# A decode block over a 537 MB cache: K and V in 4 MB tiles of 32 KB runs, wq loaded whole, w2 on 128 partitions, one K tile split into 120 and 8 partitions

## The chip, the cores and the metric

The kernel runs on one core of one Trainium2 chip. The metric is device time in microseconds (us). The kernel before takes 1334.83 us, the median of 3 runs (1334.46 to 1336.64). Two runs of this kernel that differ by less than about 0.2% can't be told apart.

An execution that is profiled has a time of its own and a span, from its first to its last instruction. Durations below come from that one execution.

## The reference

One token of each of two sequences goes through an attention block over a cache and then an MLP. All is float32.

```python
B, Sq, D = 2, 1, 512;  H, Sk, Dh = 32, 8192, 128;  F = 1792
y = layernorm(x)
q = (y @ wq) as (B, H, 1, Dh)                      # wq: D x 4096
s = einsum("bhqd,bhkd->bhqk", q, k_cache) * Dh**-0.5
o = einsum("bhqk,bhkd->bhqd", softmax(s), v_cache)
h = x + (o as (B, 1, 4096)) @ wo                   # wo: 4096 x D
z = layernorm(layernorm(h))
out = h + gelu(z @ w1 + b1) @ w2 + b2              # w1: D x F, w2: F x D
```

K and V are 268 MB each; wq and wo are 8.4 MB each, w1 and w2 3.7 MB each. Each byte is used once.

## The kernel before

**Pairs and tiles.** There are 64 pairs of a head and a sequence (`pairs`, L135). The 8192 positions of a pair lie on 128 partitions, 64 to a partition (`NS`), and are worked in two steps of 32 (`CH`, `NC` = 2). `load` (L139) fetches a step's K or V as a tile of 128 partitions x 32 positions x 128 numbers: 2 MB, in which each partition has one run of 16 KB in DRAM. All these tiles, and later w1's and w2's, come from one pool of 9 buffers (`BUFS`), used in turn: a load waits until its buffer's previous tile is done with.

**Queues.** All large loads are issued by SP in the order of the program, each for all 16 DMA engines. The loop (L235) goes over the steps. In step n it issues K of step n, now and then a wo group (`load_wo`, 2 heads, 512 KB) or a wq group (`load_wq`, 4 heads, 1 MB), and V of step n - 3 (`LAG`). The small loads of x, b1 and b2 go by ACT's queue at the start.

**Scores.** q of a head is needed on every partition. `make_q` (L119) makes it for two heads at a time: the normalised x, repeated over 128 columns (`yrep`), is the stationary side, and a slice of the wq group the moving one, so that PSUM holds q on each partition (L124, 8 matmuls a call). DVE multiplies the K tile by q in place (`multiply`, L151). ACT sums 10 of the 32 positions (`by_act`, L156), DVE the other 22 (`by_dve`, L160).

**Softmax.** After both steps of a pair: the row maximum (L167), its transpose on PE (L169), the maximum over all (L173), its spread to all partitions (L175), the exponentials on ACT (L182), and their total (L187).

**Values.** `values` (L194) multiplies the exponentials by V on PE, 8 matmuls for a tile (L199), in four groups of output rows. `gather` copies the result out of PSUM (L205); `head_sum` (L211) and `head_out` (L218) make the head's output, and `project` (L224) applies wo for a head once both sequences are done. `behind` places small DVE work after the next multiply. V of the last step comes as three loads of 16, 8 and 8 positions (L233).

**MLP.** After the loop w1 is loaded as 4 tiles of 128 rows (7 KB runs) and w2 as 4 tiles of 112 partitions (`FP`), with four runs of 2 KB to a partition (L283 to L292). The layer norms run across partitions with matmuls against a constant matrix (`layernorm_t`, L306). w1's 16 matmuls (L341) put the 1792 hidden values on four groups of partitions, 448 each; gelu (L353) is followed by four transposes on PE (L356) and a copy (L358), and w2's 16 matmuls (L362), four to a w2 tile, end in a copy (L365), a sum of the four groups (L367), the residual (L369) and the store.

Of the kernel before, what the change touches and what calls it, by code (L numbers as in the profile page):

```python
# [9 lines left out]
F32 = mybir.dt.float32  # L10
BF16 = mybir.dt.bfloat16
AF = mybir.ActivationFunctionType
ALU = mybir.AluOpType
AX = mybir.AxisListType

P = 128
EPS = 1e-5
HG = 4
QG = 2
CH = 32  # L20
NACT = 10
LAG = 3
BUFS = 9
NG = 4
WARM = 3

# [2 lines left out]
def tile_decode_block(ctx: ExitStack, tc: tile.TileContext, x, k, v, wq, wo, w1, b1, w2, b2, out):  # L29
    nc = tc.nc  # L30
    B, H, SK, DH = k.shape
    D = x.shape[-1]
    F = w1.shape[1]
    NS = SK // P
    NC = NS // CH
    DC = D // P
    FN = F // NG
    FP = FN // NG
    SCALE = DH ** -0.5

    const = ctx.enter_context(tc.tile_pool(name="const", bufs=1))
    wts = ctx.enter_context(tc.tile_pool(name="wts", bufs=2))
    kv = ctx.enter_context(tc.tile_pool(name="kv", bufs=BUFS))
    work = ctx.enter_context(tc.tile_pool(name="work", bufs=3))
    psq = ctx.enter_context(tc.tile_pool(name="psq", bufs=2, space=bass.MemoryType.PSUM))
    psm = ctx.enter_context(tc.tile_pool(name="psm", bufs=3, space=bass.MemoryType.PSUM))
# [2 lines left out]
    x2 = const.tile([B, D], F32, name="x2")  # L49
    nc.scalar.dma_start(x2, x.rearrange("b s d -> (b s) d"))  # L50

    wq_g, wo_g = {}, {}

    def load_wq(g):
        t = wts.tile([P, DC, HG * DH], F32, name="wqg")
        nc.sync.dma_start(
            t, wq[:, g * HG * DH:(g + 1) * HG * DH].rearrange("(c p) n -> p c n", p=P))
        wq_g[g] = t

    def load_wo(g):  # L60
        t = wts.tile([P, QG, D], F32, name="wog")
        nc.sync.dma_start(
            t, wo[g * QG * DH:(g + 1) * QG * DH, :].rearrange("(h p) n -> p h n", p=P))
        wo_g[g] = t

    load_wq(0)
    b1s = const.tile([NG, FN], F32, name="b1s")
    nc.scalar.dma_start(b1s, b1.rearrange("(n f) -> n f", n=NG))
    b2s = const.tile([B, D], F32, name="b2s")
# [3 lines left out]
    ident = const.tile([P, P], F32, name="ident")  # L73
# [11 lines left out]
    sel = const.tile([P, 4], F32, name="sel")  # L85
# [5 lines left out]
    so2 = [psa.tile([P, 512], F32, name=f"so{j}") for j in range(2)]  # L91
# [11 lines left out]
    y2 = const.tile([B, D], F32, name="y2")  # L103
    nc.vector.tensor_scalar(y2, x2, mv[:, 0:1], rs, op0=ALU.subtract, op1=ALU.mult)

    def transpose_rows(src):
        pt = psm.tile([P, DC, B], F32, name="sm")
        for c in range(DC):
            nc.tensor.transpose(pt[:, c, :], src[:, c * P:(c + 1) * P], ident[:B, :B])
        return pt  # L110

    ypt = transpose_rows(y2)
    yrep = const.tile([P, B, DC, P], F32, name="yrep")
    for b in range(B):
        nc.vector.tensor_copy(yrep[:, b], ypt[:, :, b:b + 1].to_broadcast([P, DC, P]))

    qps = {}

    def make_q(h):  # L119
        g, hh = divmod(h, HG)  # L120
        t = psq.tile([P, B, QG, DH], F32, name="qps")
        for b in range(B):
            for c in range(DC):
                nc.tensor.matmul(t[:, b], yrep[:, b, c, :], wq_g[g][:, c, hh * DH:(hh + QG) * DH],  # L124
                                 start=(c == 0), stop=(c == DC - 1))
        for j in range(QG):
            qps[h + j] = t[:, :, j, :]

# [5 lines left out]
    acc = psa.tile([P, DC, B], F32, name="acc")  # L134
    pairs = [(h, b) for h in range(H) for b in range(B)]  # L135
    NP = len(pairs)
    ST, PT, LT, OT = {}, {}, {}, {}

    def load(src, i, s0, n):  # L139
        h, b = pairs[i]  # L140
        t = kv.tile([P, n, DH], F32, name="kv", tag="kv")
        nc.sync.dma_start(  # L142
            t, src[b, h].rearrange("(c p j) d -> c p j d", p=P, j=CH)[s0 // CH, :, s0 % CH:s0 % CH + n])
        return t

    def multiply(i, c, kt):
        h, b = pairs[i]
        if c == 0:
            ST[i] = work.tile([P, NS], F32, name="s")
        qb = qps[h][:, b, None, :].to_broadcast([P, CH, DH])  # L150
        return nc.vector.tensor_tensor(kt, kt, qb, op=ALU.mult)  # L151

    def by_act(i, c, kt):
        s = ST[i]
        for j in range(CH - NACT, CH):
            nc.scalar.activation(kt[:, j, :], kt[:, j, :], AF.Copy,  # L156
                                 accum_out=s[:, c * CH + j:c * CH + j + 1])

    def by_dve(i, c, kt):
        nc.vector.tensor_reduce(ST[i][:, c * CH:(c + 1) * CH - NACT], kt[:, :CH - NACT, :],  # L160
                                axis=AX.X, op=ALU.add)

    MT, GM, RL, SS, OP = {}, {}, {}, {}, {}

# [29 lines left out]
    def values(i, s0, ns, vt):  # L194
        so = so2[i % 2]
        for j in range(ns // 4):
            u = s0 // 4 + j
            n = u % NG
            nc.tensor.matmul(so[32 * n:32 * n + 4], PT[i][:, 4 * u:4 * u + 4],  # L199
                             vt[:, 4 * j:4 * j + 4, :],  # L200
                             start=(u < NG), stop=(u >= NS // 4 - NG))

    def gather(i):
        SS[i] = work.tile([P, 512], F32, name="ss", bufs=2)
        nc.scalar.activation(SS[i], so2[i % 2], AF.Copy)  # L205
# [14 lines left out]
    def project(i):  # L220
        h, b = pairs[i]
        if b == B - 1:
            for c in range(DC):
                nc.tensor.matmul(acc[:, c, :], wo_g[h // QG][:, h % QG, c * P:(c + 1) * P], OT[h],  # L224
                                 start=(h == 0 and c == 0), stop=(h == H - 1),
                                 skip_group_check=True)

    def behind(m):
        return tc.issue_after(m.ins) if m is not None else nullcontext()

    kstream = [(i, c) for i in range(NP) for c in range(NC)]
    vstream = [(i, c * CH, CH) for i, c in kstream[:-1]]
    vstream += [(NP - 1, NS - CH, CH // 2), (NP - 1, NS - CH // 2, CH // 4), (NP - 1, NS - CH // 4, CH // 4)]  # L233
    maxed, expd, done, projecting = [], [], [], []
    for n in range(len(vstream) + LAG):  # L235
        live = n < len(kstream)
        if live:
            i, c = kstream[n]
            h, b = pairs[i]
            kt = load(k, i, c * CH, CH)  # L240
            if b == 0 and c == 0 and h % QG == 0:
                load_wo(h // QG)
            if b == 0 and c == 1 and h % HG == 1 and h // HG + 1 < H // HG:
                load_wq(h // HG + 1)
        if n >= LAG:
            vt = load(v, *vstream[n - LAG])
        with behind(multiply(i, c, kt) if live else None):
            for j in done:
                head_sum(j)
                head_out(j)  # L250
            for j in expd:
                inverse(j)
            for j in maxed:
                all_max(j)
        projecting, done, expd = done, [], []
        if live:
            by_act(i, c, kt)
        for j in maxed:
            exps(j)
        if live:  # L260
            by_dve(i, c, kt)
        if n >= LAG:
            iv, s0, ns = vstream[n - LAG]
            values(iv, s0, ns, vt)
        for j in maxed:
            total(j)
        expd, maxed = maxed, []
        if live and c == NC - 1:
            row_max(i)
            maxed.append(i)  # L270
            if b == 0 and h % QG == 1 and h + 1 < H:
                make_q(h + 1)
        for j in projecting:
            project(j)
        if n >= LAG and s0 + ns == NS:
            gather(iv)
            done.append(iv)
    for j in done:
        head_sum(j)
        head_out(j)  # L280
        project(j)

    w1s, w2s = [], []  # L283
    for c in range(DC):
        t = kv.tile([P, F], F32, name="w1s", tag="kv")
        nc.sync.dma_start(t, w1[c * P:(c + 1) * P, :])
        w1s.append(t)
    w2v = w2.rearrange("(n q p) d -> q p n d", p=FP, n=NG)
    for q in range(NG):
        t = kv.tile([FP, NG, D], F32, name="w2s", tag="kv")  # L290
        nc.sync.dma_start(t, w2v[q])
        w2s.append(t)  # L292

    junk = const.tile([P, 2], F32, name="junk")
    nc.scalar.activation(junk[:, 0:1], LT[NP - 1], AF.Sqrt)
# [40 lines left out]
    pf = so2[0][:, :FN]  # L336
# [12 lines left out]
    with tc.issue_after(last_ln.ins):  # L349
        nc.vector.tensor_add(hb2, hr, b2s)  # L350

    ff = work.tile([P, FN], F32, name="ff", tag="ss", bufs=2)
    nc.scalar.activation(ff, pf, AF.Gelu_apprx_tanh)  # L353
    ft = psm.tile([FP, NG, P], F32, name="sm")
    for q in range(NG):
        nc.tensor.transpose(ft[:, q, :], ff[:, q * FP:(q + 1) * FP], ident)  # L356
    fT = const.tile([FP, NG, NG, B], F32, name="fT")
    nc.vector.tensor_copy(fT, ft.rearrange("p q (n b) -> p q n b", n=NG)[:, :, :, :B])  # L358
    po = so2[1]
    for q in range(NG):  # L360
        for n in range(NG):
            nc.tensor.matmul(po[32 * n:32 * n + B], fT[:, q, n, :], w2s[q][:, n, :],  # L362
                             start=(q == 0), stop=(q == NG - 1))
    pos = work.tile([P, D], F32, name="pos", tag="ss", bufs=2)
    nc.scalar.activation(pos, po, AF.Copy)  # L365
    pr = psm.tile([B, D], F32, name="sm")
# [29 lines left out]
```

## Time and profile before

| | |
|---|---|
| median of 3 runs | 1334.83 us |
| the profiled execution, its own time | 1337.41 us |
| its span | 1335.6 us |
| read from DRAM | 561 MB, 420 GB/s over the span |
| DMA in the middle (600 to 1200 us) | 430 GB/s |
| K and V loads of 2 MB | 255, landing some 36 us after their issue |
| mean granted TensorE clock | 0.646 |

A line of the page's groups has the program's line, the engine, the operation, what it writes and reads with its shape, how often it occurs, its busy time and its mean in ns, and then how long the engine sat idle before it and what ended that. In a table of stretches, a DMA share of 1.00 means that all 16 DMA engines are occupied. A chain of work is followed back from the last instruction, at each step to what released it.

### The profile page before, as it was taken

The page shows a single profiled execution, that of the slowest core. Times are in us where ns is not written, and L with a number is a line of the kernel's source. Part 1 is how long each engine was busy: PE and PEld are TensorE (multiplying, and loading weights), DVE is VectorE, ACT ScalarE, POOL GpSimd, SP SyncE. Part 2 cuts the span into 40 slices and gives each one's busy share as a digit, 9 for nine tenths or more (in the row PEclk, how much of TensorE's full clock was granted, in tenths as well). Part 3 has the DMA queues.
Part 4 walks back from the last instruction along what each step waited for, and adds up shares of the span by engine and source line. Part 5 has one row for each costly group of instructions (what it writes and reads, how often), then busy time and mean ns, then how long its engine had stood idle before and what let it go on. Part 6 is the DMA issues. An engine that isn't in the chain of part 4 may idle for free.

```text
span 1335.6 us, 11258 instructions
## 1 busy us (share of the span) xinstructions
PE 731.0 (55%) x3501; PEld 304.1 (23%) x3502; DVE 996.3 (75%) x547; ACT 465.5 (35%) x2827; POOL 0.7 (0%) x6
## 2 busy tenths in 40 slices
PE   3465644565455565545555545564554555454566
PEld 2122211223122232221222112231221212221221
DVE  7978877777877877777787777768877777777851
ACT  2433433343333333334333333333433343343331
POOL 0000000000000000000000000000000000000000
PEclk8676566657657565566766666575676766666668
DMA  9999999999999999999999999999999999999994
GB/s 395 431 429 430 431 430 428 430 431 430 429 429 432 430 429 429 430 430 431 430 431 429 431 431 427 430 430 431 429 430 430 430 431 430 431 429 429 432 404 114
DMA packets 48239, 561.73 MB, mean 421 GB/s; under 512 B 4650, under 2 KB 4654, under 8 KB 15412
## 3 DMA queue, kind: packets, MB, share of 16 engines
q1 hardware_dynamic: 48164, 561.01, 99.1%
q8 instruction: 27, 0.44, 0.1%
q14 instruction: 32, 0.26, 0.0%
q10 hardware_dynamic: 16, 0.02, 0.0%
HBM read 561.00 MB, written 0.00 MB: 420 GB/s over the span
## 4 chain that ended last, share of the span: by engine, by line
DMA 85%; DVE 8%; PE 5%; SPq 1%; issue 1%; ACT 0%; DVEq 0%
DMA kv<-in_A_k_cache_dram 46%; DMA kv<-in_A_v_cache_dram 37%; DVE kv L151 5%; PE so L199 3%; DVE s L160 2%; DMA w2s<-in_B_w_dram 2%; PE acc L224 1%; SPq L142 1%; PE qps L124 1%; DMA wqg<-in_A_wq_dram 0%; PE so L362 0%; PE sm L367 0%; DVE ot L218 0%; PE sm L169 0%; ACT L182 0%
## 5 line engine op out<-in xcount | busy, mean ns | idle before, releaser
L151 DVE TENSOR_TENSOR kv<-kv,qps 128x4096 f32<-128x4096 f32 x128 | 565.9, 4421 | 290.3 <-DMA kv<-in_A_k_cache_dram 285.0
L156 ACT ACTIVATE kv<-kv 128x128 f32<-128x128 f32 x1280 | 376.1, 295 | 786.2 <-DVE kv L151 786.2
L199 PE MATMUL so<-kv,pt 128*4 128x512 f32 x2048 | 424.7, 974 | 137.2 <-DMA kv<-in_A_v_cache_dram 137.2
L160 DVE TENSOR_REDUCE s<-kv 128x22 f32<-128x2816 f32 x128 | 392.4, 3066 | 0.1
L156 ACT ACTIVATION_READ_ACCUMULATOR kv<-kv 128x1 f32 x1280 | 238.9, 187 | 0.0
L175 PE MATMUL sm<-gm,srow 1*128 1x1 f32 x128 | 34.1, 333 | 254.6 <-DVE gm L173 254.5
L199 PEld LDWEIGHTS so<-kv,pt 128*4 128x4 f32 x2048 | 51.4, 104 | 322.6 <-issue 179.6
L124 PE MATMUL qps<-wqg,yrep 128*128 128x256 f32 x256 | 82.6, 465 | 49.6 <-issue 24.8
L211 PE MATMUL sm<-sel,ss 128*128 128x1 f32 x512 | 84.5, 286 | 18.8 <-ACT ss L205 18.7
L175 PEld LDWEIGHTS sm<-gm,srow 1*128 1x128 f32 x128 | 28.7, 277 | 283.0 <-DVE gm L173 282.0
L224 PE MATMUL acc<-ot,wog 128*128 128x2 f32 x256 | 56.7, 343 | 59.7 <-DVE ot L218 59.7
L211 PEld LDWEIGHTS sm<-sel,ss 128*128 128x128 f32 x512 | 79.1, 236 | 25.9 <-ACT ss L205 25.9
L224 PEld LDWEIGHTS acc<-ot,wog 128*128 128x128 f32 x256 | 58.6, 326 | 63.8 <-DVE ot L218 61.3
L124 PEld LDWEIGHTS qps<-wqg,yrep 128*128 128x128 f32 x256 | 54.4, 232 | 55.7 <-issue 49.6
L169 PE MATMUL sm<-ident,mx 128*1 128x128 f32 x64 | 21.4, 334 | 64.7 <-DVE mx L167 64.7
L205 ACT ACTIVATE ss<-so 128x512 f32<-128x512 f32 x64 | 38.2, 597 | 48.5 <-PE so L199 47.7
L187 PEld LDWEIGHTS sm<-ls,ones 128*128 128x128 f32 x128 | 25.2, 246 | 96.7 <-ACT pt L182 91.8
L169 PEld LDWEIGHTS sm<-ident,mx 128*1 128x1 f32 x64 | 5.1, 79 | 155.2 <-DVE mx L167 103.7
L187 PE MATMUL sm<-ls,ones 128*128 128x1 f32 x128 | 30.6, 308 | 3.8 <-ACT pt L182 3.2
L182 ACT ACTIVATE pt<-s,nb 128x64 f32<-128x64 f32 x64 | 22.3, 348 | 2.1
L218 DVE TENSOR_SCALAR ot<-sm,rl 128x1 f32<-128x1 f32 x64 | 13.6, 212 | 11.6 <-PE sm L211 11.6
L173 DVE TENSOR_REDUCE gm<-sm 1x1 f32<-1x128 f32 x64 | 17.4, 272 | 2.4 <-PE sm L169 2.4
(70 smaller groups left out, 87.1 us busy)
## 6 DMA issues: line engine op xcount, KB each, us to landing
kv<-in_A_k_cache_dram SPq DMA_DIRECT2D x128, 2048.0 KB, 36.3
kv<-in_A_v_cache_dram SPq DMA_DIRECT2D x127, 2048.0 KB, 35.9
wqg<-in_A_wq_dram SPq DMA_DIRECT2D x8, 1024.0 KB, 36.8
wog<-in_A_wo_dram SPq DMA_DIRECT2D x16, 512.0 KB, 35.2
w1s<-in_B_w_dram SPq DMA_DIRECT2D x4, 896.0 KB, 28.3
w2s<-in_B_w_dram SPq DMA_DIRECT2D x4, 896.0 KB, 23.5
kv<-in_A_v_cache_dram SPq DMA_DIRECT2D x1, 1024.0 KB
kv<-in_A_v_cache_dram SPq DMA_DIRECT2D x2, 512.0 KB, 31.1
```

The costliest lines, as they stand in the source:

```text
L124: nc.tensor.matmul(t[:, b], yrep[:, b, c, :], wq_g[g][:, c, hh * DH:(hh + QG) * DH], start=(c == 0), stop=(c == DC - 1))
L151: return nc.vector.tensor_tensor(kt, kt, qb, op=ALU.mult)
L156: nc.scalar.activation(kt[:, j, :], kt[:, j, :], AF.Copy, accum_out=s[:, c * CH + j:c * CH + j + 1])
L160: nc.vector.tensor_reduce(ST[i][:, c * CH:(c + 1) * CH - NACT], kt[:, :CH - NACT, :], axis=AX.X, op=ALU.add)
L169: nc.tensor.transpose(MT[i], mx, ident)
L175: nc.tensor.matmul(GM[i], srow, gm, start=True, stop=True)
L182: nc.scalar.activation(pt, ST.pop(i), AF.Exp, bias=nb, scale=SCALE, accum_out=ls)
L187: nc.tensor.matmul(RL[i], ones, LT[i], start=True, stop=True)
L199: nc.tensor.matmul(so[32 * n:32 * n + 4], PT[i][:, 4 * u:4 * u + 4], vt[:, 4 * j:4 * j + 4, :], start=(u < NG), stop=(u >= NS // 4 - NG))
L205: nc.scalar.activation(SS[i], so2[i % 2], AF.Copy)
L211: nc.tensor.matmul(OP[i], ss[:, j * DH:(j + 1) * DH], sel[:, j:j + 1], start=(j == 0), stop=(j == 3))
L224: nc.tensor.matmul(acc[:, c, :], wo_g[h // QG][:, h % QG, c * P:(c + 1) * P], OT[h], start=(h == 0 and c == 0), stop=(h == H - 1), skip_gr ...
```

## The change

- **Tiles.** A pair's K or V is one tile of 4 MB, in which a partition holds 64 consecutive positions: one run of 32 KB. The pool has 5 such buffers instead of 9 of 2 MB. The two steps of a pair remain, as halves of the K tile. K of the next pair is issued a pair ahead, V of a pair after it; the matmuls with V of pair i - 1 stand in the second step of pair i. The last pair's K comes as 2 loads, its V as 3.
- **K of pair 62**, the last but one, comes as a load of partitions 0 to 119 and a load of 120 to 127 (`PS`).
- **q.** All of wq is loaded ahead of K, as two 4 MB tiles of the same pool with 32 KB runs. Partition p has rows 4p to 4p + 3 of wq, and x is transposed to match. 32 matmuls of 512 columns make q for all heads at once; two ACT copies put it into SBUF (`q2`), and `make_q` spreads two heads with a 0/1 matrix (`pick`), one matmul for each sequence instead of four.
- **wo** groups keep their size; the load of the next group stands in the step before its first head.
- **w1** is one tile with 4 loads. **w2** is one tile on 128 partitions, partition p holding rows 14p to 14p + 13, in loads of 4, 4, 4 and 2 rows: runs of 8 KB (the last 4 KB). gelu writes its output in the order that 32 x 32 transposes on DVE need, and these replace the four transposes on PE and the copy; w2 takes 14 matmuls instead of 16.

```diff
-HG = 4
+PS = 120
+WG = 2
-LAG = 3
-BUFS = 9
+BUFS = 5
...
+    FT = F // P
...
+    wqv = wq.rearrange("(p r) n -> p r n", r=DC)
+    wqs = []
+    for r in range(0, DC, 2):
+        t = kv.tile([P, 2, H * DH], F32, name="wqs", tag="kv")
+        nc.sync.dma_start(t, wqv[:, r:r + 2, :])
+        wqs += [t[:, 0, :], t[:, 1, :]]
...
+    ypt = psm.tile([P, DC, B], F32, name="sm")
+    for r in range(DC):
+        nc.tensor.transpose(ypt[:, r, :], y2.rearrange("b (p r) -> b r p", r=DC)[:, r, :], ident[:B, :B])
+    yT = const.tile([P, DC, B], F32, name="yT")
+    nc.vector.tensor_copy(yT, ypt)
+    pick = const.tile([P, B, P], F32, name="pick")
+    nc.vector.tensor_copy(pick, sel[:, :B, None].to_broadcast([P, B, P]))
+    QW = H * DH // NG
+    q2 = const.tile([P, QW], F32, name="q2")
+    for r in range(DC):
+        for j in range(QW // 512):
+            for n in range(NG):
+                nc.tensor.matmul(so2[j][32 * n:32 * n + B], yT[:, r, :],
+                                 wqs[r][:, n * QW + j * 512:n * QW + (j + 1) * 512],
+                                 start=(r == 0), stop=(r == DC - 1))
+    for j in range(QW // 512):
+        nc.scalar.activation(q2[:, j * 512:(j + 1) * 512], so2[j], AF.Copy)
...
     def make_q(h):
-        g, hh = divmod(h, HG)
+        n, at = divmod(h * DH, QW)
         t = psq.tile([P, B, QG, DH], F32, name="qps")
         for b in range(B):
-            for c in range(DC):
-                nc.tensor.matmul(t[:, b], yrep[:, b, c, :], wq_g[g][:, c, hh * DH:(hh + QG) * DH],
-                                 start=(c == 0), stop=(c == DC - 1))
+            nc.tensor.matmul(t[:, b], pick[32 * n:32 * n + B, b, :],
+                             q2[32 * n:32 * n + B, at:at + QG * DH], start=True, stop=True)
...
-    def load(src, i, s0, n):
+    def load(src, i, parts):
         h, b = pairs[i]
-        t = kv.tile([P, n, DH], F32, name="kv", tag="kv")
-        nc.sync.dma_start(
-            t, src[b, h].rearrange("(c p j) d -> c p j d", p=P, j=CH)[s0 // CH, :, s0 % CH:s0 % CH + n])
+        t = kv.tile([P, NS, DH], F32, name="kv", tag="kv")
+        for s0, n in parts:
+            rows = src[b, h].rearrange("(p j) d -> p j d", j=NS)
+            for p0, p1 in [(0, PS), (PS, P)] if src is k and i == NP - 2 else [(0, P)]:
+                nc.sync.dma_start(t[p0:p1, s0:s0 + n], rows[p0:p1, s0:s0 + n])
         return t
...
-    kstream = [(i, c) for i in range(NP) for c in range(NC)]
-    vstream = [(i, c * CH, CH) for i, c in kstream[:-1]]
-    vstream += [(NP - 1, NS - CH, CH // 2), (NP - 1, NS - CH // 2, CH // 4), (NP - 1, NS - CH // 4, CH // 4)]
+    whole = [(0, NS)]
+    kt, vt = {}, {}
+    kt[0] = load(k, 0, whole)
+    load_wo(0)
+    steps = [(i, c) for i in range(NP) for c in range(NC)] + [(NP, 0), (NP, 1)]
+    for i, c in steps:
+        live = i < NP
+        if c == 0:
+            if live:
+                h, b = pairs[i]
+            if i + 1 < NP:
+                kt[i + 1] = load(k, i + 1, whole if i + 1 < NP - 1 else [(0, CH), (CH, CH)])
+            if live and b == 1 and (h + 1) % WG == 0 and h + 1 < H:
+                load_wo((h + 1) // WG)
+            if live:
+                vt[i] = load(v, i, whole if i < NP - 1 else [(0, CH), (CH, CH // 2), (CH + CH // 2, CH // 2)])
...
-        if n >= LAG:
-            iv, s0, ns = vstream[n - LAG]
-            values(iv, s0, ns, vt)
+        if c == 1 and i > 0:
+            values(i - 1, 0, NS, vt.pop(i - 1))
...
+    w1t = kv.tile([P, DC, F], F32, name="w1s", tag="kv")
     for c in range(DC):
-        t = kv.tile([P, F], F32, name="w1s", tag="kv")
-        nc.sync.dma_start(t, w1[c * P:(c + 1) * P, :])
+        nc.sync.dma_start(w1t[:, c, :], w1[c * P:(c + 1) * P, :])
-    w2v = w2.rearrange("(n q p) d -> q p n d", p=FP, n=NG)
-    for q in range(NG):
-        t = kv.tile([FP, NG, D], F32, name="w2s", tag="kv")
-        nc.sync.dma_start(t, w2v[q])
+    w2v = w2.rearrange("(p t) d -> p t d", t=FT)
+    w2t = kv.tile([P, FT, D], F32, name="w2s", tag="kv")
+    for t in range(0, FT, NG):
+        nc.sync.dma_start(w2t[:, t:min(t + NG, FT), :], w2v[:, t:min(t + NG, FT), :])
...
-    ff = work.tile([P, FN], F32, name="ff", tag="ss", bufs=2)
-    nc.scalar.activation(ff, pf, AF.Gelu_apprx_tanh)
-    ft = psm.tile([FP, NG, P], F32, name="sm")
-    for q in range(NG):
-        nc.tensor.transpose(ft[:, q, :], ff[:, q * FP:(q + 1) * FP], ident)
-    fT = const.tile([FP, NG, NG, B], F32, name="fT")
-    nc.vector.tensor_copy(fT, ft.rearrange("p q (n b) -> p q n b", n=NG)[:, :, :, :B])
+    ff = work.tile([P, FT, 32], F32, name="ff", tag="ss", bufs=2)
+    nc.scalar.activation(ff, pf.rearrange("p (u t) -> p t u", t=FT), AF.Gelu_apprx_tanh)
+    fT = const.tile([P, FT, 32], F32, name="fT")
+    nc.vector.transpose(fT.rearrange("p t r -> p (t r)"), ff.rearrange("p t u -> p (t u)"))
     po = so2[1]
-    for q in range(NG):
-        for n in range(NG):
-            nc.tensor.matmul(po[32 * n:32 * n + B], fT[:, q, n, :], w2s[q][:, n, :],
-                             start=(q == 0), stop=(q == NG - 1))
+    for t in range(FT):
+        n = t % NG
+        nc.tensor.matmul(po[32 * n:32 * n + B], fT[:, t, :B], w2t[:, t, :],
+                         start=(t < NG), stop=(t >= FT - NG))
```

More of the change, by code (lines that the diff above doesn't have):

```diff
@@ L37, in tile_decode_block @@
     FN = F // NG
-    FP = FN // NG
+    FT = F // P
     SCALE = DH ** -0.5
@@ L50, in tile_decode_block, with load_wo @@
     nc.scalar.dma_start(x2, x.rearrange("b s d -> (b s) d"))
-    wq_g, wo_g = {}, {}
-    def load_wq(g):
-        t = wts.tile([P, DC, HG * DH], F32, name="wqg")
+    wo_g = {}
+    def load_wo(g):
+        t = wts.tile([P, WG, D], F32, name="wog")
         nc.sync.dma_start(
[L57 to L61, printed above, removed]
-        nc.sync.dma_start(
-            t, wo[g * QG * DH:(g + 1) * QG * DH, :].rearrange("(h p) n -> p h n", p=P))
-        wo_g[g] = t
-    load_wq(0)
+            t, wo[g * WG * DH:(g + 1) * WG * DH, :].rearrange("(h p) n -> p h n", p=P))
+        wo_g[g] = t
+    wqv = wq.rearrange("(p r) n -> p r n", r=DC)
[4 more added lines that the diff above has]
+        wqs += [t[:, 0, :], t[:, 1, :]]
     b1s = const.tile([NG, FN], F32, name="b1s")
@@ L110, in transpose_rows @@
         return pt
[L112 to L115, printed above, removed]
+    ypt = psm.tile([P, DC, B], F32, name="sm")
[15 more added lines that the diff above has]
+        nc.scalar.activation(q2[:, j * 512:(j + 1) * 512], so2[j], AF.Copy)
     qps = {}
     def make_q(h):
-        g, hh = divmod(h, HG)
+        n, at = divmod(h * DH, QW)
         t = psq.tile([P, B, QG, DH], F32, name="qps")
         for b in range(B):
-            for c in range(DC):
-                nc.tensor.matmul(t[:, b], yrep[:, b, c, :], wq_g[g][:, c, hh * DH:(hh + QG) * DH],
-                                 start=(c == 0), stop=(c == DC - 1))
+            nc.tensor.matmul(t[:, b], pick[32 * n:32 * n + B, b, :],
+                             q2[32 * n:32 * n + B, at:at + QG * DH], start=True, stop=True)
         for j in range(QG):
@@ L137, in tile_decode_block @@
     ST, PT, LT, OT = {}, {}, {}, {}
-    def load(src, i, s0, n):
+    def load(src, i, parts):
         h, b = pairs[i]
-        t = kv.tile([P, n, DH], F32, name="kv", tag="kv")
-        nc.sync.dma_start(
-            t, src[b, h].rearrange("(c p j) d -> c p j d", p=P, j=CH)[s0 // CH, :, s0 % CH:s0 % CH + n])
+        t = kv.tile([P, NS, DH], F32, name="kv", tag="kv")
[3 more added lines that the diff above has]
+                nc.sync.dma_start(t[p0:p1, s0:s0 + n], rows[p0:p1, s0:s0 + n])
         return t
@@ L150, in multiply @@
         qb = qps[h][:, b, None, :].to_broadcast([P, CH, DH])
-        return nc.vector.tensor_tensor(kt, kt, qb, op=ALU.mult)
+        kc = kt[:, c * CH:(c + 1) * CH, :]
+        return nc.vector.tensor_tensor(kc, kc, qb, op=ALU.mult)
     def by_act(i, c, kt):
         s = ST[i]
-        for j in range(CH - NACT, CH):
-            nc.scalar.activation(kt[:, j, :], kt[:, j, :], AF.Copy,
-                                 accum_out=s[:, c * CH + j:c * CH + j + 1])
+        for j in range((c + 1) * CH - NACT, (c + 1) * CH):
+            nc.scalar.activation(kt[:, j, :], kt[:, j, :], AF.Copy, accum_out=s[:, j:j + 1])
     def by_dve(i, c, kt):
-        nc.vector.tensor_reduce(ST[i][:, c * CH:(c + 1) * CH - NACT], kt[:, :CH - NACT, :],
-                                axis=AX.X, op=ALU.add)
+        a, e = c * CH, (c + 1) * CH - NACT
+        nc.vector.tensor_reduce(ST[i][:, a:e], kt[:, a:e, :], axis=AX.X, op=ALU.add)
     MT, GM, RL, SS, OP = {}, {}, {}, {}, {}
@@ L199, in values @@
             nc.tensor.matmul(so[32 * n:32 * n + 4], PT[i][:, 4 * u:4 * u + 4],
-                             vt[:, 4 * j:4 * j + 4, :],
+                             vt[:, 4 * u:4 * u + 4, :],
                              start=(u < NG), stop=(u >= NS // 4 - NG))
@@ L223, in project @@
             for c in range(DC):
-                nc.tensor.matmul(acc[:, c, :], wo_g[h // QG][:, h % QG, c * P:(c + 1) * P], OT[h],
+                nc.tensor.matmul(acc[:, c, :], wo_g[h // WG][:, h % WG, c * P:(c + 1) * P], OT[h],
                                  start=(h == 0 and c == 0), stop=(h == H - 1),
@@ L229, in behind @@
         return tc.issue_after(m.ins) if m is not None else nullcontext()
-    kstream = [(i, c) for i in range(NP) for c in range(NC)]
-    vstream = [(i, c * CH, CH) for i, c in kstream[:-1]]
-    vstream += [(NP - 1, NS - CH, CH // 2), (NP - 1, NS - CH // 2, CH // 4), (NP - 1, NS - CH // 4, CH // 4)]
+    whole = [(0, NS)]
     maxed, expd, done, projecting = [], [], [], []
[L235 to L244, printed above, removed]
-        if n >= LAG:
-            vt = load(v, *vstream[n - LAG])
-        with behind(multiply(i, c, kt) if live else None):
+    kt, vt = {}, {}
[13 more added lines that the diff above has]
+                vt[i] = load(v, i, whole if i < NP - 1 else [(0, CH), (CH, CH // 2), (CH + CH // 2, CH // 2)])
+        with behind(multiply(i, c, kt[i]) if live else None):
             for j in done:
@@ L256, in tile_decode_block @@
         if live:
-            by_act(i, c, kt)
+            by_act(i, c, kt[i])
         for j in maxed:
@@ L260, in tile_decode_block @@
         if live:
-            by_dve(i, c, kt)
-        if n >= LAG:
-            iv, s0, ns = vstream[n - LAG]
-            values(iv, s0, ns, vt)
+            by_dve(i, c, kt[i])
+        if c == 1 and i > 0:
+            values(i - 1, 0, NS, vt.pop(i - 1))
         for j in maxed:
@@ L274, in tile_decode_block @@
             project(j)
-        if n >= LAG and s0 + ns == NS:
-            gather(iv)
-            done.append(iv)
+        if c == 1 and i > 0:
+            gather(i - 1)
+            done.append(i - 1)
     for j in done:
@@ L281, in tile_decode_block @@
         project(j)
-    w1s, w2s = [], []
+    w1t = kv.tile([P, DC, F], F32, name="w1s", tag="kv")
     for c in range(DC):
-        t = kv.tile([P, F], F32, name="w1s", tag="kv")
-        nc.sync.dma_start(t, w1[c * P:(c + 1) * P, :])
-        w1s.append(t)
-    w2v = w2.rearrange("(n q p) d -> q p n d", p=FP, n=NG)
-    for q in range(NG):
-        t = kv.tile([FP, NG, D], F32, name="w2s", tag="kv")
-        nc.sync.dma_start(t, w2v[q])
-        w2s.append(t)
+        nc.sync.dma_start(w1t[:, c, :], w1[c * P:(c + 1) * P, :])
+    w1s = [w1t[:, c, :] for c in range(DC)]
+    w2v = w2.rearrange("(p t) d -> p t d", t=FT)
+    w2t = kv.tile([P, FT, D], F32, name="w2s", tag="kv")
+    for t in range(0, FT, NG):
+        nc.sync.dma_start(w2t[:, t:min(t + NG, FT), :], w2v[:, t:min(t + NG, FT), :])
     junk = const.tile([P, 2], F32, name="junk")
```

## The prediction

> **What bounds the kernel now.** I read the page from the top: the busy row, the DMA row in 40 slices, the queues, and then the chain that ended last.
>
> ```profile
> PE 731.0 (55%) x3501; PEld 304.1 (23%) x3502; DVE 996.3 (75%) x547; ACT 465.5 (35%) x2827; POOL 0.7 (0%) x6
> ...
> DMA  9999999999999999999999999999999999999994
> ...
> q1 hardware_dynamic: 48164, 561.01, 99.1%
> q8 instruction: 27, 0.44, 0.1%
> ...
> q10 hardware_dynamic: 16, 0.02, 0.0%
> ...
> DMA 85%; DVE 8%; PE 5%; SPq 1%; issue 1%; ACT 0%; DVEq 0%
> ...
> L151 DVE TENSOR_TENSOR kv<-kv,qps 128x4096 f32<-128x4096 f32 x128 | 565.9, 4421 | 290.3 <-DMA kv<-in_A_k_cache_dram 285.0
> ```
>
> The 16 DMA engines are busy in every slice, the chain is DMA for 85%, and DVE, the busiest engine, idles 285 us for K. So bytes set the middle. The last 40 us are another matter; the table of stretches (busy us of PE, PEld, DVE, ACT, POOL, then granted clock, DMA share, GB/s) shows it:
>
> ```profile
> 600.00:1200.00 600.00, 328.65 (x1568) 136.81 (x1572) 459.25 (x240) 213.11 (x1315) 0.00 (x0) 0.64 1.01 430
> 1305.00:1312.00 7.00, 5.36 (x32) 3.25 (x31) 1.84 (x11) 0.89 (x2) 0.00 (x0) 1.00 1.04 220
> 1321.00:1328.00 7.00, 3.54 (x28) 0.53 (x26) 0.54 (x2) 0.00 (x0) 0.00 (x0) 0.98 0.08 30
> ```
>
> Two things stand there. From 1321 to 1328 us a share of 0.08 at 30 GB/s is about one engine of 16: **one engine is late**, and the kernel waits for it alone. And from 1305 to 1312 all engines are occupied at half the bytes (220 against 430): something **slows the packets** there. The chain in order of time says that this stretch is on the path:
>
> ```profile
> 1299.52 5.27 PE so L199 x29
> 1304.79 23.47 DMA w2s<-in_B_w_dram
> 1328.26 0.04 issue
> 1328.30 1.93 PE so L362 x8
> ```
>
> The last w2 piece lands at 1328.3, and 7.3 us of work follow to the span's end at 1335.6 (L362 to 1330.2, the copy pos 0.6, L367's matmuls 1.9, res 0.7, and 2.1 for the store).
>
> The trace also keeps, for every load, when each of the 16 engines reported its share. The last engine is 2.1 us behind the first at 98 us, 5.5 at 499, 9.5 at 902 and 13.6 at 1269, in steps of some 0.6 us about every 45 us. That is the rhythm of q8's 27 fetches of 16 KB (27 x 0.6 = 16 us). The second-latest engine is 6.4 us behind at 1269. So one engine carries the instruction fetches beside its data; it sets the landing of every load.
>
> **The sum.** It follows this late engine.
>
> *Packets.* In the middle, eight K/V loads of 2 MB take 38.90 us; seven and one wo load 35.32; seven and one wq load 36.60. That gives 4.863 us for an engine's 8 packets of 16 KB (0.608 each), 1.28 for the 16 packets of 2 KB of wo, and 2.56 for the 32 of wq (0.080 each). So a packet costs about 0.0046 us plus 0.0368 us a KB. By that, 7 KB cost 0.268, 8 KB 0.306, 32 KB 1.211. K and V are 2048 packets of 16 KB an engine now, 1024 of 32 KB then, if a 32 KB run is one packet: 1024 x 0.0046 = 4.7 us less, and half the reports; I take -5 (bounds: 0 if the run is cut in two, -9 by the packets' own recorded times, 611 ns for 16 KB and 309 for 8 KB). wq: 8 x 2.56 = 20.5 now, 16 x 1.211 = 19.4 then: -1.1. L124's 512 PE instructions (256 matmuls, 256 weight loads) become about 256, which is one 16 KB fetch fewer: -0.6. Together -6.7 before the last V part.
>
> *The tail's slow stretch.* The late engine ends V's last 512 KB at 1304.1; its own lag of 13.5 over the first engine's 1288.7 would put it at 1302.2. Then the four w1 loads end at 1308.8, 1313.2, 1316.7 and 1319.1, though 32 packets of 7 KB cost 8.6 us by the sum above: 1302.2 + 8.6 = 1310.8, so 8.3 us are lost. In the packet records w1's take 272 ns until w2's begin at 1298 and some 500 while both are in flight; w2's own take 130 to 180 against 84 ns when the late engine is alone. K, V, wo and wq loads mix sizes all through the kernel without this, at 430 GB/s; what only w2 has is 112 partitions, 7 to an engine instead of 8. [...] w2 itself is 4 x 2.24 = 9 us from 1319.1 to 1328.3, and 28 x 0.306 = 8.6 after.
>
> So without the 120/8 split, the last w2 piece lands at 1302.2 - 6.7 + 8.6 + 8.6 = 1312.7, 15.6 us earlier.
>
> *The 120/8 split.* No load of 120 partitions is in this trace, so I bound it. Best: the late engine gets none of those 120 rows, 8 x 1.211 = 9.7 us of relief; then the second-latest decides, 7.1 us earlier than the late one, plus one row of 32 KB (1.2): -5.9. Worst: no relief, and all engines are slowed as w2's were. Nearest row: w2's 140 ns against 84 while the engines were out of step, 1.67 times; on 9.7 us that is +6.5 (twice, as w1's 272 to 500, is +9.7). [...] Relief and slowing together: the late engine is freed, the 15 others come 6.5 + 1.2 us later from a start 7.1 earlier: +0.6. I take that, 1313.3, and keep -6 and +8 as ends.
>
> [...]
>
> *The compute tail.* It must keep up. Counted back from the last w2 landing E: V's last part lands at E - 17.2, V of pair 62 at E - 27, K of pair 63 at E - 36.7. DVE needs 2 x (4.42 + 3.07) = 15 us a pair. K 62 lands at E - 56 and is done at E - 41; K 63's halves are done at E - 33.5 and E - 26, and the softmax (4.5 us from L160 to the values now) is through by E - 18, since the values of pair 62 (7.2 us at half clock) stand ahead on PE. Values of 63: 16 matmuls, 3.8 us, to about E - 14. Now 8.7 us lie between these (1304.8) and the first w1 matmul (1313.5), then 4 x 0.93 for w1, 1.67 for gelu and fT (the DVE transpose replaces 0.65 of PE and 0.19 of DVE; nearest row: L350's 0.68 for 512 columns; taken equal), and 14 w2 matmuls, 3.6. That ends at E + 4. After it 0.6 + 0.9 + 0.7 + 2.1 us: E + 8. If DMA decides, the last piece has 2 matmuls instead of 4: 7.3 - 1.0 = 6.3. I take E + 7.3, as now: compute has caught up with DMA, so further gains on E alone would not all count.
>
> *The start.* DVE's first multiply moves from 12.0 us to about 33 (wq 8.4 MB, then K 4.2 MB, at 430 GB/s, and 3 us of ramp). It costs nothing as long as DVE catches up: it needs 15.6 of the 19.5 us a pair has, and waits for K by the second pair. The 32 q matmuls and 2 copies (7 + 1.2 us) lie under K 0's landing. Buffers: five of 4 MB. SP queues V n behind K n-1's release. K n-1 is done 15.6 us after landing, and V n's turn comes after four loads of 9.7 us, 39 us: 23 to spare, 10 for the engine that is furthest ahead. K n waits for V n-4, 32 to spare. Were that cover gone, every us of it would count 60 times.
>
> Span: 1313.3 + 7.3 = 1320.6, or 15.0 less than 1335.6. The profiled execution took 1337.41 with its 1335.6 of span; the median of the runs shown is 1334.83. Off the median: **1320 us**.
>
> **The rivals.**
> 1. *As summed*, the split about neutral: 1316 to 1324. Chance 0.50.
> 2. *The split frees the late engine and slows nobody*: E = 1306.8. Compute then ends it; its chain hangs on V's last part, which comes as much earlier: 1313 to 1315. For: the lag is one engine's. Against: w2's slowing. Chance 0.20.
> 3. *The split slows and frees nobody*: E = 1319 to 1322, so 1326 to 1329. Chance 0.12.
> 4. *The change does not do what it says*: the runs are cut into 16 KB packets (+5), or the slow stretch comes from w1 beside w2 and not from 112 partitions (+8): 1325 to 1333. Against the second: w2's last load, started by all engines together at 1317, ran at 84 to 104 ns. Chance 0.10.
> 5. *Slower*: runs spaced 32 KB apart read more slowly than those 16 KB apart. Place: each K and V packet; 1250 us of the span. From a loss of 1.2% (15 of 1250 us, 15 ns a packet) it eats the gain; at 3% it is 37 us: 1357. Against: rows 2 KB apart (wo) and 16 KB apart (wq) cost the same 0.080 us a packet. Chance 0.05. [...]
>
> The remaining 0.03 is a gain lost to something unseen, within 0.2%, about what a measurement of this kernel can tell from no change. So faster 0.92, same 0.03, slower 0.05. The range leaves out the slow end of rival 4 and rival 5, and takes in rivals 2 and 3: 1311 to 1329.
>
> **What would show it.** K and V as 32 KB packets of about 1.21 us, and some 16,400 of them; GB/s in the middle 431 to 432. w1 and w2 landing 2.2 us apart with no slow stretch. At the load of 120, the late engine's lag falling from 13.5 to about 4, and the others' rising by some 6. After the last landing 6 to 8 us. Wrong would be: DVE waiting over 0.3 us more a pair for K with DMA below a share of 0.99 (buffers), or packets above 1.23 us (rival 5).

## The result, and the profile after

The changed kernel takes 1366.54 us (median of 4 runs, 1364.26 to 1368.49), the kernel before 1335.05: 1.023 times as long, 95% interval 1.0217 to 1.0242. The forecast was 1320, faster. The profiled execution has a span of 1364.4 us.

The page of the changed kernel, with the same lines as were shown of before (busy time; DMA in 40 slices and its GB/s; the queue; the chain by engine and by line; the multiply):

```profile
PE 633.1 (46%) x3365; PEld 265.7 (19%) x3366; DVE 993.7 (73%) x547; ACT 466.4 (34%) x2829; POOL 0.7 (0%) x6
...
DMA  9999999999999999999999999999999999999972
GB/s 406 433 430 431 431 429 431 430 431 431 430 430 430 430 430 430 430 431 430 429 431 429 432 430 431 431 429 431 430 430 430 431 430 430 429 428 273 336 307 85
...
q1 hardware_dynamic: 24667, 561.00, 97.5%
...
DMA 69%; DVE 19%; PE 9%; another core or an unknown queue 2%; issue 0%; ACT 0%; SPq 0%; DVEq 0%
...
L166 DVE TENSOR_TENSOR kv<-kv,qps 128x4096 f32<-128x4096 f32 x128 | 564.4, 4410 | 327.8 <-DMA kv<-in_A_k_cache_dram 327.8
```

The GB/s row of the kernel before, for comparison:

```profile
GB/s 395 431 429 430 431 430 428 430 431 430 429 429 432 430 429 429 430 430 431 430 431 429 431 431 427 430 430 431 429 430 430 430 431 430 431 429 429 432 404 114
```

Two lines tell most of it. The GB/s of the changed kernel stay near 430 for 36 slices, as before, and then fall to 273 although the DMA row above them still says 9. And DVE waits 43 us more for K than before (327.8 against 285.0). The number of packets has halved, so the 32 KB runs are single packets: the trace has 16,384 of them, 97% of those before 1230 us recorded at 1213 to 1225 ns.

The table of stretches of the changed kernel shows where the bytes went:

```profile
600.00:1200.00 600.00, 283.15 (x1498) 121.19 (x1498) 461.91 (x240) 214.49 (x1320) 0.00 (x0) 0.63 1.00 430
1200.00:1236.00 36.00, 15.00 (x77) 7.20 (x81) 28.69 (x15) 11.88 (x77) 0.00 (x0) 0.61 1.01 432
1240.00:1272.00 32.00, 4.12 (x21) 3.74 (x20) 15.40 (x8) 7.13 (x44) 0.00 (x0) 0.54 1.01 199
```

Up to 1236 us nothing is wrong. From 1240 to 1272 all engines are occupied (1.01) and move less than half (199 of 430). That is when the K tile of pair 62 is under way, the one that was split into 120 and 8 partitions. In the packet records of this stretch a 32 KB packet takes about 2.5 us instead of 1.216, with single ones up to 3.7.

The chain of the changed kernel in order of time (start, duration, what) gives the price:

```profile
1199.40 49.44 DMA kv<-in_A_k_cache_dram
...
1248.93 4.42 DVE kv L166
...
1261.07 3.05 DVE s L175
...
1264.43 29.79 another core or an unknown queue
...
1294.30 4.42 DVE kv L166
```

DVE is done with K of pair 61 at 1264.4 and then stands still for 29.8 us, until the second part of pair 62's K has landed at 1294.2. (The view cannot name a wait for two loads into one tile, and writes "an unknown queue".) K of pairs 62 and 63 then costs DVE 30.7 us, and a tail of 39 us follows.

The reports of the single engines show whom the split hit. In the changed kernel the 120-partition load had one report at once and 15 later, the last at 1292.0 us; the 8-partition load had 8, the last at 1294.2. The late engine is the last in both. So one engine was left out of the 120 partitions, but not the late one. The engine that was left out reported its share of the next V at 1260, 16 us ahead of all others.

### The profile page after: what moved, and what is told of

It is laid out like the page before. It is cut to its first block, busy times and chain, and to the rows that moved or that the text cites. A ratio compares the mean times of both kernels' runs of the same rounds, so it can differ in the third digit from the quotient of the medians.

```text
span 1364.4 us, 10682 instructions
## 1 busy us (share of the span) xinstructions
PE 633.1 (46%) x3365; PEld 265.7 (19%) x3366; DVE 993.7 (73%) x547; ACT 466.4 (34%) x2829; POOL 0.7 (0%) x6
## 4 chain that ended last, share of the span: by engine, by line
DMA 69%; DVE 19%; PE 9%; another core or an unknown queue 2%; issue 0%; ACT 0%; SPq 0%; DVEq 0%
DMA kv<-in_A_k_cache_dram 49%; DMA kv<-in_A_v_cache_dram 21%; DVE kv L166 12%; PE so L213 7%; DVE s L175 7%; PE qps L136 1%; PE so L371 0%; PE so L353 0%; DVE gm L187 0%; PE so L350 0%; DVE ot L232 0%; PE sm L225 0%; DVE rl L205 0%; PE wp L316 0%
## 5 line engine op out<-in xcount | busy, mean ns | idle before, releaser
L166 DVE TENSOR_TENSOR kv<-kv,qps 128x4096 f32<-128x4096 f32 x128 | 564.4, 4410 | 327.8 <-DMA kv<-in_A_k_cache_dram 327.8
L213 PE MATMUL so<-kv,pt 128*4 128x512 f32 x2048 | 369.2, 887 | 92.8 <-DMA kv<-in_A_v_cache_dram 92.8
L213 PEld LDWEIGHTS so<-kv,pt 128*4 128x4 f32 x2048 | 59.9, 111 | 353.7 <-issue 256.9
L201 PE MATMUL sm<-ls,ones 128*128 128x1 f32 x128 | 37.5, 362 | 119.0 <-ACT pt L196 119.0
L225 PE MATMUL sm<-sel,ss 128*128 128x1 f32 x512 | 67.3, 253 | 22.1 <-ACT ss L219 21.9
L225 PEld LDWEIGHTS sm<-sel,ss 128*128 128x128 f32 x512 | 61.9, 191 | 37.3 <-ACT ss L219 37.2
L201 PEld LDWEIGHTS sm<-ls,ones 128*128 128x128 f32 x128 | 32.0, 311 | 125.3 <-ACT pt L196 125.3
L136 PE MATMUL qps<-q,pick 2*128 2x256 f32 x64 | 28.3, 539 | 49.8 <-DVE rl L205 49.8
L183 PE MATMUL sm<-ident,mx 128*1 128x128 f32 x64 | 17.5, 273 | 33.7 <-DVE mx L181 33.6
L232 DVE TENSOR_SCALAR ot<-sm,rl 128x1 f32<-128x1 f32 x64 | 13.6, 212 | 16.6 <-PE sm L225 16.6
L136 PEld LDWEIGHTS qps<-q,pick 2*128 2x128 f32 x64 | 12.4, 237 | 53.4 <-issue 50.5
L181 DVE TENSOR_REDUCE mx<-s 128x1 f32<-128x64 f32 x64 | 14.1, 220 | 6.5
```

Of the source, the lines that this page charges most:

```text
L136: nc.tensor.matmul(t[:, b], pick[32 * n:32 * n + B, b, :], q2[32 * n:32 * n + B, at:at + QG * DH], start=True, stop=True)
L166: return nc.vector.tensor_tensor(kc, kc, qb, op=ALU.mult)
L183: nc.tensor.transpose(MT[i], mx, ident)
L201: nc.tensor.matmul(RL[i], ones, LT[i], start=True, stop=True)
L225: nc.tensor.matmul(OP[i], ss[:, j * DH:(j + 1) * DH], sel[:, j:j + 1], start=(j == 0), stop=(j == 3))
```

## The experiments

All ratios are to the kernel before, run beside them on the same chip; intervals are 95%.

**Theories.** A: the split alone costs the time; my guess at why, which no run shows, was that rows of a load that has not 128 partitions do not lie on the engines as in the other loads. B: the larger tiles, fewer buffers or the new order cost it. C: the uneven share (15 engines, then 8) costs it.

**e1: no split.** In the changed kernel:

```diff
-            for p0, p1 in [(0, PS), (PS, P)] if src is k and i == NP - 2 else [(0, P)]:
+            for p0, p1 in [(0, P)]:
```

> The changed kernel with K of pair 62 as one load of 128 partitions again. Theory A (the 120/8 split alone did the harm, since its rows do not lie on the engines as 128 partitions do): K of pair 62 lands about 31 us sooner, near 1263 instead of 1294 us; DVE is done with K of the last pair near 1293 instead of 1325; the same compute tail of 39 us follows, so a span of 1330 to 1335, near the kernel before (1335). Theory B (five 4 MB buffers or the new order of loads cost it): it stays above 1355. If my forecast's other terms held in full, it would be near 1320.

Measured: 1335.07 us, ratio 0.9995 (0.9986 to 1.0005), span 1333.7. K of pair 62 lands at 1263.4, 30.9 us sooner, and the time falls by 31.5. B is out as the cause of the 31 us. Nor is it that a tile comes in two loads: K of pair 63 does so here, each of 128 partitions, and each takes its 4.9 us. But the kernel without the split is only as fast as the one before: some 15 us of forecast gain are missing, and that is a question of its own, taken up from e4 on.

**e2: the split alone, in the kernel before.**

```diff
+        rows = src[b, h].rearrange("(c p j) d -> c p j d", p=P, j=CH)[s0 // CH, :, s0 % CH:s0 % CH + n]
+        for p0, p1 in [(0, 120), (120, P)] if src is k and i == NP - 2 else [(0, P)]:
+            nc.sync.dma_start(t[p0:p1], rows[p0:p1])
```

> The kernel before with nothing changed but K of pair 62: each of its two 2 MB loads as 120 and 8 partitions. Theory A: packets in flight double to about 1.2 us while those loads run, the late engine loses 20 to 30 us, and the time is 1350 to 1365. Theory B: no change, 1335.

Measured: 1361.77 us, 1.0194 (1.0177 to 1.0211): some 25 us lost with nothing else changed, and 16 KB packets of about 1.2 us in the stretch (0.611 otherwise). As A has it.

**e3: 112 and 16 partitions.** In the changed kernel `PS = 112`. Both 112 and 16 divide by 16.

> The changed kernel with the split at 112 instead of 120 partitions; both parts can be shared out evenly over 16 engines, 7 rows and 1 row each. Theory A (rows that do not lie as in a 128-partition load): as slow as the change or nearly, 1345 to 1370, with 32 KB packets of 2 to 2.5 us around 1240 to 1270. Theory C (the uneven share, 15 engines and then 8, is what costs): near the run without a split.

Measured: 1361.51 us, 1.0195 (1.018 to 1.0211). The stretch of slow bytes is there as before, 195 GB/s at a DMA share of 1.04:

```profile
1243.00:1267.00 24.00, 2.97 (x12) 2.78 (x12) 15.40 (x8) 6.55 (x43) 0.00 (x0) 0.54 1.04 195
```

In the same 24 us the kernel without a split (e1) moved 424 GB/s:

```profile
1243.00:1267.00 24.00, 10.18 (x53) 4.78 (x53) 19.01 (x9) 7.16 (x44) 0.00 (x0) 0.61 0.99 424
```

C is out as the main cause, if the 16 engines shared both parts evenly. The tile still lands 4.4 us earlier than in the change (1289.8 against 1294.2); whether that is the share of 15 engines and then 8, no run says.

**e8: 64 and 64 partitions.** `PS = 64`, to ask what about the rows costs.

> The changed kernel with K of pair 62 as two loads of 64 partitions, 4 rows to each of 16 engines. [...]

Measured: 1360.79 us, 1.0179 (1.0164 to 1.0194). The packets took about 2.5 us, near the 2.4 that I expected, and from 1243 to 1267 us 203 GB/s were moved (e1: 424). The loss is 25 us; my estimate was 10 to 14, a time of 1343 to 1352, with the engines at half speed for this tile. Against e1 the other engines finish this tile some 15 us late, the late one 25. It is slowed before its own turn, on loads of 128 partitions, while the others are at the odd load: K of pair 61 comes 5.4 us late, and V of pair 60 adds 9.8. I had priced the tile's packets alone.

Shown is that a tile with such rows slows itself, 2.5 us a packet over 1.216 or 2.1 times, and the loads beside it. Why it does was not shown: no trace here says which engine writes where.

**e4: w2 alone on 128 partitions, in the kernel before** (the change's w2 loads, gelu order, DVE transposes and 14 matmuls, nothing else).

> The kernel before with w2 alone on 128 partitions (8 KB runs, DVE transposes, 14 matmuls). My term (the slow stretch comes from 112 partitions): w1's packets stay at 272 ns, the last w2 piece lands near 1320 instead of 1328, and the time is 1325 to 1329. Rival (w1 beside w2 is slow in any layout): 1332 to 1336.

Measured: 1346.52 us, 1.008 (1.0065 to 1.0095): slower, outside both expectations. The table of stretches pointed away from the tail: the middle had become slower too, 423 to 429 GB/s in its slices instead of about 430, and eight K/V loads took 39.15 us instead of 38.90. Nothing in the loop had changed. What had changed is where the buffers lie: `fT` grew from 128 to 1792 bytes a partition, and it is allocated ahead of them. By the allocation of the built programs the K/V buffers start at 0 modulo 256 bytes in the kernel before, at 128 in e4 and at 160 in the changed kernel; the sizes of the constants agree, which put them 1664 and 2720 bytes further on. Theory D, from these three starts: a buffer off a multiple of 256 bytes makes each packet longer.

**e5: only the padding, in the kernel before.**

```diff
+    pad = const.tile([P, 32], F32, name="pad")
+    nc.vector.memset(pad, 0.0)
     sel = const.tile([P, 4], F32, name="sel")
```

> The kernel before with one unused constant of 128 bytes a partition ahead of the pools, so that each K/V buffer starts at 128 instead of 0 modulo 256 in its partition. Theory D (the run with w2 on 128 partitions lost its gain because its larger constants moved the buffers off a multiple of 256 bytes; each 16 KB packet took some 3.7 ns more): 39.14 us for eight 2 MB loads instead of 38.90, and 1342 to 1348. Rival (the w2 layout itself did it): 1335, unchanged.

Measured: 1349.26 us, 1.0091 (1.0076 to 1.0106). A constant that nobody reads costs 12 us; the time lies 1 us above the range expected. The middle of this kernel:

```profile
600.00:1200.00 600.00, 333.85 (x1555) 141.90 (x1547) 452.32 (x236) 208.66 (x1282) 0.00 (x0) 0.62 1.01 427
```

427 instead of 430 GB/s; a 2 MB load takes 4.894 us instead of 4.862, 16 KB packets are recorded at 611 to 622 ns instead of 611 flat. 256 loads x 0.032 = 8.2 us; most of the rest is the late engine, 16.6 us behind the first on the last V loads instead of 13.5.

**e6: e4 with the buffers back on 256 bytes** (the same two lines, 128 bytes, in e4).

> The kernel before with w2 on 128 partitions, and 128 bytes of padding that put the K/V buffers back on a multiple of 256. Theory D: 38.90 us for eight loads as before, w1's packets at 272 ns, last w2 piece near 1320, and 1325 to 1330. Rival (the layout): 1342 to 1348 again.

Measured: 1331.96 us, 0.9962 (0.9947 to 0.9977). Loads at 4.862 again; w1's packets stay at 272 ns throughout, with w2's in flight beside them; the last w2 piece lands at 1319.3 instead of 1328.3. So my term for the slow stretch holds: it came from the layout of w2. e6 changes w2's partitions and its runs (2 KB to 8 KB) together; that the 112 partitions did it is argued from wo, whose 2 KB runs on 128 partitions pass through the middle without such a stretch (430 GB/s), and from e3 (195 GB/s with parts of 112 and 16). Of these 9 us the time shows about 5, short of the 1325 to 1330 expected: the compute chain now ends 12.6 us after the last landing instead of 7.3.

**e7: the changed kernel without the split, buffers on 256 bytes** (e1 and 96 bytes of padding).

> The changed kernel without the split, and with 96 bytes of padding (its K/V buffers start at 160 modulo 256, then at 0). Theory D: a 4 MB load takes 9.68 to 9.69 us instead of 9.715, K of pair 62 lands 3 to 4 us sooner, and the time is 1330 to 1332, the compute tail of 39 us unchanged. Rival (32 KB packets are limited otherwise): 1335.

Measured: 1327.24 us, 0.9923 (0.9906 to 0.9939), faster than both kernels. A 4 MB load takes 9.681 us. The middle:

```profile
600.00:1200.00 600.00, 282.42 (x1498) 121.22 (x1498) 465.86 (x241) 214.31 (x1320) 0.00 (x0) 0.64 1.00 432
```

K of pair 62 lands at 1255.6, 7.8 us before e1, more than I expected: 0.034 x 128 = 4.4 us from the packets, 2.9 from the late engine's lag, 12.4 instead of 15.3. The last w2 piece lands at 1312.1. Yet the span ends at 1325.7, 13.6 later: from the end of DVE's work on K there are 39 us again, as expected. The chain of e7 in order of time says why:

```profile
1283.17 3.05 DVE s L177
...
1286.58 0.37 PE sm L185
1286.95 6.34 PE so L215 x32
...
1295.02 0.31 PE sm L191 x2
1295.33 1.01 PE so L352 x2
1296.34 0.52 PE sm L203 x2
1296.86 1.59 PE so L352 x6
1298.45 5.72 PE so L215 x32
...
1312.44 3.19 PE so L355 x32
```

No DMA is in it behind K. The last softmax (L185 to L203) has the values of pair 62 (L215, 6.34 us) in the middle of it, since they stand there in PE's order of work; L352 are the matmuls that put b1 in. w1's matmuls (L355) start at 1312.4, though the last w1 piece landed at 1303.5.

**e9: V one pair later.** Since DVE and that chain hang on the last K, I gave K a start: V of a pair is loaded and used one pair later, so that three V tiles follow the last K instead of two.

```diff
-            if live:
-                vt[i] = load(v, i, whole if i < NP - 1 else [(0, CH), (CH, CH // 2), (CH + CH // 2, CH // 2)])
+            if 1 <= i <= NP:
+                vt[i - 1] = load(v, i - 1, whole if i < NP else [(0, CH), (CH, CH // 2), (CH + CH // 2, CH // 2)])
...
-        if c == 1 and i > 0:
-            values(i - 1, 0, NS, vt.pop(i - 1))
+        if c == 1 and i > 1:
+            values(i - 2, 0, NS, vt.pop(i - 2))
```

> The changed kernel without the split, with the 96 bytes of padding, and with V of a pair loaded and used one pair later, so that the last K lands 9.7 us sooner against the end. Theory E (after the split and the padding, the end is set by the compute chain behind the last K: DVE done at 1286, values of pair 62 ahead of the last softmax on PE, 39 us to the end): DVE is done near 1277, the last w2 piece lands at 1312 as before, and the end follows it by some 6 us: span 1318 to 1320, time 1319 to 1322. Rival (the tail behind w2 is as long in any order): 1327, unchanged.

Measured: 1321.17 us (5 runs, 1320.88 to 1325.21), 0.9903 (0.9887 to 0.992), the lowest of all, though its interval overlaps that of e7. DMA is on the path of its last stretch again, and 6.9 us lie between the last w2 piece (1312.5) and the end (1319.4):

```profile
1261.55 29.00 DMA kv<-in_A_v_cache_dram
1290.55 0.04 issue
1290.60 1.02 PE so L215 x2
1291.62 0.98 PE sm L227 x8
```

**e10: the change with the padding alone.** Split and all, 96 bytes more.

> The change as it is, split and all, with the 96 bytes of padding alone. Theories A and D together (split +31 us, buffers off a multiple of 256 bytes +8): 1356 to 1361. Rival (the split only costs where the buffers are misplaced): near 1327.

Measured: 1359.22 us, 1.0176 (1.0158 to 1.0194): 32 to 34 us over e7, and K of pair 62 lands 33.0 us later than there. So the split costs as much with the buffers on 256 bytes. The misplaced buffers cost 7 us with the split and 10 without: within some 3 us the two losses add up.

**e11: where the late engine stands.** e7, and in pairs 41 to 48 a load of 1 to 8 rows of 256 bytes by the same queue.

> The changed kernel without the split, with padding (buffers on a multiple of 256), and in pairs 41 to 48 one more load of 1 to 8 partitions, 256 bytes each, that nothing waits for. It finds the late engine's place: if small loads go one row to an engine from the first on, loads of more rows than its number report some 8 to 10 us after their other rows, those of fewer do not. The 8-partition part of the split waited for the late engine, so I expect it among the first 8. Time within 1 us of the run without these loads, 1327.

Measured: 1329.96 us (one execution, span 1328.2), 2.7 over e7 where 1 was expected. The load of one row reported in step with the first engines (850.1 us, 0.7 behind the first). The load of two rows reported at 869.5 and at 877.8, 8.3 us apart; each larger one had its last report 9 to 10 us behind its first. So if rows go to the engines from the first on, the late engine is the second. None of the loads of 2 to 8 rows passes it by.

## Why the prediction was wrong, point by point

**The 120/8 split: the step that failed.** It said: the late engine is freed, the 15 others come 6.5 + 1.2 us later, +0.6 in all, with -6 and +8 as ends. Measured: +31 us on the landing (e1 against the change) and on the time. Three things were wrong in it. *Whom it frees*: no row of before shows which engine is late, or that a load of 120 partitions leaves one out, and yet I took the good case as the value. In the run one engine was left out (15 reports, and one at once), and it was not the late one. *The factor*: 2.1 instead of w2's 1.67; the 8 partitions took the late engine 2.2 us and not 1.2. *Its reach*, which mattered most: I multiplied the tile's own 9.7 us. The slow stretch begins when the first engine comes to the odd load and ends when the last one leaves it, and the engines are 14.6 us apart by then. The late engine's reports show the sum: K of pair 61 comes 4.9 us later than in e1, V of pair 60 takes 23.7 us instead of 9.7, the 120 partitions 19.5 instead of 9.7, the 8 partitions 2.2. 4.9 + 14.0 + 9.8 + 2.2 = 30.9. The end of the range was a bound on one load's packets, not on what the load does to its neighbours. The third rival (the split slows and frees nobody, chance 0.12) had the right kind of thing, at +6 to +9 us instead of +31. Nor did I name this as the rival for slower; the one I named (runs 32 KB apart read slowly) did not occur: 9.681 us for 4 MB.

**The packets: right, but for a condition that I did not see.** -5 us was forecast for K and V. With the buffers on 256 bytes it is (2 x 4.862 - 9.681) x 128 = 5.5; in the change as made, with 9.715, it is 1.2. The missing 4.3, and some 3 us of lag, went to buffers that start 160 bytes past a multiple of 256. No row of before could show this, since all its buffers lie alike; the size of each constant is in the code. (The price of 0.0368 us a KB is right for a KB of 1000 bytes.)

**The slow stretch in the tail: right.** e6 shows it apart from the rest: w1 at 272 ns, the last w2 piece 9.0 us sooner. I had 8.3 + 0.4. Why w2's 112 partitions should slow the packets, no run shows. And without the split the last w2 piece was forecast for 1312.7; e7 has 1312.1, e1 1320.5.

**The compute tail: mis-sized.** I took E + 7.3; e7 has E + 13.6. I had the values of 63 done by E - 14; they end at 1304.2, E - 7.9. In my count the values of pair 62 began when their V landed (E - 27), some 2 us of softmax followed, and the values of 63 took 3.8. On PE the row maximum of the last pair (L185) stands ahead of them and waits for DVE until E - 25.5. Behind them come 5.2 us of softmax, of copying and summing for pair 62 (L221, L227) and of b1 (L352), and the values of 63 take 5.72. So in e1 and e7 6 us of the gain went there, and e9, which takes the chain away from the last K, has E + 6.9. With that, most of the 15 us missing in e1 is found: its last w2 piece lands 7.8 us later than forecast, by the offset of the buffers, and its end lies 5.9 us further behind.

**The late engine's steps: misread.** I took them for the rhythm of q8's fetches of 16 KB, and a fetch fewer for -0.6 us. Between 100 and 1230 us the kernel before has 19 steps of 0.6 to 1.0 us, some 56 us apart and not 45. A step lies between two reports of the late engine, some 5 us apart. By the packet records one of q8's 23 fetches in that time falls into 2 of these 19 gaps, and a fetch of 8 KB on another queue into all 19 (ten more of that queue fall outside):

```profile
q14 instruction: 32, 0.26, 0.0%
```

In e7, with reports some 10 us apart, it is 18 of 19 for q14 and 2 for q8. So no row stands behind the -0.6, though the fetch fewer came (q8: 26 in the change, 27 before). What the runs show is that the steps come together with q14's fetches; no run moved those.

**The start and the buffers: right.** DVE's first multiply is at 32.5 us instead of 12.0, and costs nothing that shows, as the last landing of e7 (1312.1 for 1312.7) has it; between 600 and 1200 us the changed kernel has the same 430 GB/s at a DMA share of 1.00, with five buffers.

## What to carry to other kernels

A tile loaded in other shares of the partitions than its neighbours (120/8, 112/16 and 64/64 beside 128) slowed not only itself here: with the loads in flight beside it all engines moved 187 to 203 GB/s in these stretches (the change, e3, e8, e10) instead of some 430, so one odd tile of 4 MB cost 25 to 33 us. Before trying to relieve a late DMA engine, ask which one it is, with loads of 1, 2, 3 rows (in e11 the two reports of the load of two rows came 8.3 us apart). And where a kernel is bound by DMA, look at the address of its buffers whenever the size of a constant changes (128 bytes cost 12 us in e5).

## What the runs showed of the hardware

- An offset of 128 bytes in the start of the buffers cost 0.032 us for a 2 MB load (4.862 to 4.894) and 12 us in all (e5); an offset of 160 bytes 0.034 us for 4 MB in 32 KB packets (9.681 to 9.715). The source stayed where it was and only the place in SBUF moved. Shifts of 1792 bytes (e6) and 2816 (e7), both multiples of 256 and not of 512, leave the loads at 4.862 and 9.681 us; those of 128 (e5), 1664 (e4) and 2720 (the change) do not. Why the offset costs time was not shown, and why the late engine falls behind by 3 us more as well is open.
- In the change the load of 120 partitions had one report at once and 15 later, the last at 1292.0 us; the load of 8 had 8, the last at 1294.2.
- One engine falls behind by 0.6 to 1.0 us about every 56 us, each time with an instruction fetch of 8 KB on queue q14 (19 of 19 steps between 100 and 1230 us in the kernel before); e11 puts it second, if rows go to the engines from the first on. That these fetches cause the lag was not tried by itself.
